# Wider idle matmuls, a split query load and one priority per step in a planned attention + MLP kernel

## The chip, the cores and the metric

One core of a Trainium2 chip. The metric is the device time of one execution in microseconds (us); every time below is of that kind or comes from one profiled execution. The engines are TensorE (PE, with PEld for its weight loads), VectorE (DVE), ScalarE (ACT), GpSimd (POOL) and SyncE (SP); they run side by side and wait for each other through semaphores. POOL issues the loads, SP the stores.

## The reference

```
batch, heads, seq, head_dim = 8, 8, 576, 64;  n_pack = 32
def sm_attn(qq, kk, vv):                     # softmax(qq kk^T / 8) vv
    ...
p_packed = sm_attn(p, k, v)                  # 32 packed rows per head
out = sm_attn(q, p_packed, p_packed)         # 576 rows per head
x = out.transpose(0, 2, 1, 3).reshape(8 * 576, 512)
r = maximum(x @ w_in, 0)                     # w_in 512 x 2048
result = (r * r) @ w_out                     # w_out 2048 x 512, float32
```

Inputs are float32; the kernel computes in bf16 with float32 sums.

## The kernel before

The kernel goes through the eight batches one after the other, with the eight heads of a batch in two halves of four ("qd" 0 and 1). A batch is a chain of steps, each with a short name, then the batch, then an index:

- `Lk`, `Lv`, `Lq`: loads of keys, values, queries, with a cast from float32 to bf16 on the way. `LWI.c.i` are the two halves of the four column chunks of w_in (order entries a0 to a3), `LWO.c` the eight chunks of two 128-row blocks of w_out (b0 to b7), `LP.2` the packed p of batches 2 to 7 (p2). Each is one `dma_start` on POOL.
- `Tk`, `Tq` (and `TR` for the rest of batch 0's queries): transposes on DVE (L458, L451, L455). `P`, `X`: p transposed and spread into block diagonals.
- `S1`: scores of p with the keys (PE, L467 to L482), then maximum (DVE, L490), exponential (ACT, L494), normalisation (DVE). `E`: transposes of it (PE, L507) and a copy. `PV`: times the values (PE, L521 and L541). `XT`: the packed rows copied out, turned and spread by small matmuls, and four small block copies into `pq_bd` (L373 on ACT or L375 on DVE).
- `S2` (for batch 0 `SA`, `SB`, `SC`; `ST`, `C` and `N` behind it): scores of q with the packed rows (PE, L629), transposes, maximum, subtraction, exponential, sum, product, transposes back.
- `M` (`MX`, `MY`, `MZ`): packed rows times w_in (PE, L596), so that the second attention's result need not be multiplied by w_in in full, and copies to SBUF.
- `F1` (batch 0: `FA` for its first 256 tokens, `F1` for the other 320): attention weights times `M` (PE, L782 and L795), relu (ACT mostly, L820 and L804), square (DVE mostly, L830).
- `F2.t.fb`: 128 tokens (tile t) times block fb of w_out (PE, L838, 512 columns, one matmul each), summed in one PSUM bank over fb 0 to 15; behind fb 15 a copy to `o_sb` and the stores. F2 blocks 2c and 2c+1 need load `LWO.c`. The last tile is done in three column parts (L855).

Nothing in this order is decided on the chip. While the program is built, the class `Plan` runs a list scheduler (`forward`, L68): streams of steps, a rough duration for each piece and engine, buffers and PSUM banks that must be free, and for every load a transfer time and a lag until it counts as landed (L894 to L904, L1117). Of the steps that can start, that with the lowest priority number goes first. The number is a step's base level plus an offset from the table `TABLE` (L248), looked up by the step's key (L205), which is the name up to the batch, so that all 16 matmuls of an F2 tile share one offset; a second table leans single pieces to or from ACT. Each engine then gets its instructions in the planned order and executes them strictly in that order.

Loads are issued in the order of `ORDER` (L1124), as far as the priorities leave it; at most eight are under way (the slot "dq", L874): the ninth is issued when the first has landed. Where the plan sees PE idle before the first F2, `fills` (L238) puts in matmuls on zeros into PSUM bank 7 (`keep_clock`, L357), 70 of them of 256 columns. The early lines of `ORDER`, up to `EARLY`, are streams of their own; the rest is one stream.

Of the kernel before, what the change touches and what calls it, by code (L numbers as in the profile page):

```python
# [53 lines left out]
class Plan:  # L54
# [147 lines left out]
    def aim(self):  # L202
        for steps in self.streams:
            for st in steps:
                st.prio = self.prio.get(st.key, self.level(st))  # L205
                st.late = st.prio - (50.0 if st.key[:2] == "F2" else 0.25)
                if st.key[0] == "L":
                    st.late = -200.0
                for stage in st.pieces:
                    for pc in stage:  # L210
                        pc.lean = self.lean.get(f"{st.key}/{pc.stage}", 0.0)
# [29 lines left out]
    def use(self, z):  # L241
        level = {st.key: self.level(st) for steps in self.streams for st in steps}
        self.prio = {k: level[k] + d for k, d in z.get("o", {}).items() if k in level}
        self.lean = z.get("l", {})
        self.wait, self.margin = z.get("w", 0.0), z.get("m", 0.0)


TABLE = {'o': {'P.0': 12.64, 'X.0': -182.5, 'P.2': 786.53, 'X.1': 824.47, 'La0': -989.93, 'La1': -654.2, 'La2':  # L248
# [54 lines left out]


def kernel_impl(tc, q, k, v, p, w_in, w_out, out):
# [922 lines left out]
```

## Time and profile before

| | |
|---|---|
| timed runs | 249.72 us median of 3 (249.71 to 249.84) |
| the profiled execution | 249.95 us, its span 248.2 us |
| granted TensorE clock, mean | 1.00 |
| PE busy | 234.0 us (94%), of which idle matmuls L359: 70 of 0.32 us |
| DVE, ACT, POOL busy | 193.1, 163.5, 43.0 us |
| chain that ended last, by engine | PE 71%, DMA 17%, DVE 4%, ACT 2% |
| F2, L838 | 509 records, 133.5 us |
| F1 of batches 1 to 7, L782 | 448 matmuls, 71.8 us; its relu on ACT 112 of 0.65 us, its square on DVE 112 of 0.46 us |
| load queue of POOL | 18.55 MB |

Busy times are unions: a matmul's record reaches beyond the start of the next one, so 0.379 us is the record of an F2 matmul and 0.213 us the distance to the next. A few per cent of the matmul records are missing, which shows as a gap of one matmul. The chain of waits is followed back from the last instruction, and a DMA piece in it lasts from issue to landing, with its time in the queue. The 40 slices of the page show where the load queue is full:

```profile
PE   7789799899999999999999999999999999999992
PEld 5465365356544654366544664466544654465452
DVE  7788989998799868996799669996799769756200
ACT  7457788969856597659756892567565793779110
POOL 8834544433343230000000000000000000000000
PEclk9999999999999999999999999999999999999999
DMA  6999999999999999702023111220032003310222
```

A digit is the busy share of 6.2 us in tenths. DMA is full for the first 16 slices, up to some 99 us; PE falls below 9 only in the first eight and the last.

### The profile page before, as it was taken

To read this page: it belongs to the slowest core of one execution; us is meant where nothing else is said; L and a number is where in the kernel's file an instruction comes from. 1 tells how busy PE (TensorE), PEld (TensorE's weight loads), DVE (VectorE), ACT (ScalarE), POOL (GpSimd) and SP (SyncE) were. 2 spreads that over 40 slices of the span, in tenths; PEclk is the share of its full clock that TensorE was granted. 3 is DMA by queue.
4 is the path that set the end of the run, shared out by engine and by line. 5 is a ranking of instruction groups with operands and counts; after the bars stand their busy time and mean duration, and the time that the engine had idled before them with its cause. 6 is when DMAs were issued, how large, how long until landed. Compare 5 with 4: busy or idle time off the path is not lost.

```text
span 248.2 us, 5863 instructions
## 1 busy us (share of the span) xinstructions
PE 234.0 (94%) x2315; PEld 129.9 (52%) x2350; DVE 193.1 (78%) x368; ACT 163.5 (66%) x284; POOL 43.0 (17%) x76
## 2 busy tenths in 40 slices
PE   7789799899999999999999999999999999999992
PEld 5465365356544654366544664466544654465452
DVE  7788989998799868996799669996799769756200
ACT  7457788969856597659756892567565793779110
POOL 8834544433343230000000000000000000000000
PEclk9999999999999999999999999999999999999999
DMA  6999999999999999702023111220032003310222
GB/s 106 202 191 207 202 203 203 203 228 241 223 220 224 237 217 207 189 21 66 0 66 80 29 42 43 57 64 13 3 87 66 21 0 85 86 44 0 68 72 75
DMA packets 26715, 28.50 MB, mean 115 GB/s; under 512 B 5440, under 2 KB 18112, under 8 KB 26688
## 3 DMA queue, kind: packets, MB, share of 16 engines
q0 software_dynamic: 18960, 18.55, 45.5%
q1 hardware_dynamic: 6960, 9.32, 13.6%
q8 instruction: 18, 0.29, 0.5%
q10 hardware_dynamic: 768, 0.26, 0.4%
q14 instruction: 9, 0.07, 0.1%
HBM read 37.22 MB, written 9.44 MB: 188 GB/s over the span
## 4 chain that ended last, share of the span: by engine, by line
PE 71%; DMA 17%; DVE 4%; issue 2%; POOL 2%; ACT 2%; SPq 0%; ACTq 0%; DVEq 0%; POOLq 0%
PE pb L838 41%; PE ps L782 21%; DMA w_in_b<-in_moe_w_in_dram 8%; DMA q_b<-in_q_dram 4%; DMA w_out_b<-in_moe_w_out_dram 4%; PE ps L596 2%; PE ps L482 1%; PE pb L507 1%; PE ps L629 1%; ACT r L820 1%; PE pb L521 1%; PE pb L629 1%; DMA out_dram<-o_sb 1%; DVE gT L830 1%; DVE n L753 1%
## 5 line engine op out<-in xcount | busy, mean ns | idle before, releaser
L838 PE MATMUL pb<-w_out_b,gT 128*128 128x512 bf16 x509 | 133.5, 379 | 3.1 <-issue 0.8
L838 PEld LDWEIGHTS <-gT 128*128 128x128 bf16 x560 | 51.9, 97 | 61.3 <-issue 6.5
L820 ACT ACTIVATE r<-ps 128x576 bf16<-128x576 f32 x112 | 71.9, 654 | 14.9 <-PE ps L782 10.3
L782 PE MATMUL ps<-a,M 128*128 128x288 bf16 x448 | 71.8, 286 | 0.4 <-ACT r L820 0.2
L830 DVE TENSOR_TENSOR gT<-r 128x576 bf16<-128x576 bf16 x112 | 50.8, 456 | 25.8 <-ACT r L820 24.7
L782 PEld LDWEIGHTS <-M 128*128 128x128 bf16 x448 | 43.1, 98 | 19.9 <-issue 1.4
L373 ACT COPY o_sb<-pb 128x512 f32<-128x512 f32 (+1 forms) x20 | 11.0, 555 | 24.0 <-PE pb L838 20.4
L373 ACT CAST M<-ps 128x1024 bf16<-128x1024 f32 (+1 forms) x20 | 19.2, 969 | 10.2 <-PE ps L596 10.1
L375 DVE COPY o_sb<-pb 128x512 f32<-128x512 f32 (+1 forms) x17 | 11.3, 662 | 10.8 <-PE pb L855 10.2
L494 ACT ACTIVATE e1x<-ps,n 128x576 bf16<-128x576 f32 x16 | 11.8, 739 | 10.5 <-DVE n L490 10.4
L741 ACT ACTIVATE e<-d 128x1152 bf16<-128x1152 f32 (+2 forms) x9 | 9.1, 1009 | 11.3 <-DVE d L736 11.3
L458 DVE STREAM_TRANSPOSE kT<-k_b 128x576 f32<-128x576 f32 x16 | 12.0, 775 | 2.3 <-DMA k_b<-in_k_dram 2.2
L428 POOL DMA_DIRECT2D v_b<-in_v_dram x16 | 11.2, 701 | 13.1 <-DMA k_b<-in_k_dram 5.7
L359 PE MATMUL pb<-zero 128*128 128x256 bf16 x70 | 11.7, 319 | 1.1 <-DVE zero L378 1.1
L490 DVE TENSOR_REDUCE n<-ps 128x1 f32<-128x576 f32 x16 | 11.5, 747 | 0.6 <-PE ps L482 0.5
L423 POOL DMA_DIRECT2D q_b<-in_q_dram x16 | 8.9, 562 | 17.1 <-DVE kT L458 5.2
L747 DVE TENSOR_REDUCE t<-e 128x36 f32<-128x1152 bf16 (+2 forms) x9 | 10.3, 1148 | 1.4 <-ACT e L741 1.4
L423 POOL DMA_DIRECT2D k_b<-in_k_dram x16 | 8.7, 543 | 13.5 <-DVE gT L830 3.3
L373 ACT CAST M<-pb 128x512 bf16<-128x512 f32 x18 | 9.9, 596 | 1.3 <-PE pb L596 1.3
L753 DVE TENSOR_TENSOR n<-e,r 128x1152 bf16<-128x1152 bf16 (+2 forms) x9 | 10.5, 1165 | 0.3
L451 DVE STREAM_TRANSPOSE qT<-q_b 128x576 f32<-128x576 f32 x14 | 10.7, 767 | 0.0
L645 DVE STREAM_TRANSPOSE a<-n 128x576 bf16<-128x576 bf16 (+1 forms) x14 | 10.1, 743 | 0.1
(103 smaller groups left out, 239.1 us busy)
## 6 DMA issues: line engine op xcount, KB each, us to landing
out_dram<-o_sb SPq DMA_DIRECT2D x141, 64.0 KB, 1.7
k_b<-in_k_dram POOLq DMA_DIRECT2D x16, 288.0 KB, 12.1
q_b<-in_q_dram POOLq DMA_DIRECT2D x16, 288.0 KB, 11.7
v_b<-in_v_dram POOLq DMA_DIRECT2D x8, 320.0 KB, 11.7
v_b<-in_v_dram POOLq DMA_DIRECT2D x8, 256.0 KB, 11.5
w_in_b<-in_moe_w_in_dram POOLq DMA_DIRECT2D x8, 256.0 KB, 10.8
w_out_b<-in_moe_w_out_dram POOLq DMA_DIRECT2D x8, 256.0 KB, 10.5
p_b<-in_p_dram POOLq DMA_DIRECT2D x1, 192.0 KB, 10.6
```

The costliest lines, as they stand in the source:

```text
L359: nc.tensor.matmul(half(7)[:, :2 * P], lhsT=zero[:, :P], rhs=zero, start=True, stop=True)
L373: nc.scalar.copy(dst, src)
L375: eng.tensor_copy(dst, src)
L423: nc.gpsimd.dma_start(t, src[self.b, qd * QH:(qd + 1) * QH].rearrange("h (a j) d -> (h a) (j d)", j=JT))
L458: nc.vector.transpose(kT[:, qd].rearrange("p s x -> p (s x)").bitcast(F32).rearrange("p (x a j2) -> p j2 x a", a=32, j2=2), self.t.k[qd][: ...
L490: nc.vector.tensor_reduce(self.n1[:, qd:qd + 1], self.ps1[qd], axis=AX.X, op=ALU.max, negate=True)
L494: nc.scalar.activation(e1x[:, qd], self.ps1[qd], ACT.Exp, bias=self.n1[:, qd:qd + 1], accum_out=self.d1[:, qd:qd + 1])
L753: eng.tensor_tensor(out=self.n2[:, g0:g1], in0=self.e2[:, g0:g1], in1=self.r2[:, g0:g1].unsqueeze(2).to_broadcast([P, g1 - g0, 32]), op=AL ...
L782: nc.tensor.matmul(ps[:, c], lhsT=a.M[:, qd, fb * FB:(fb + 1) * FB], rhs=a.a2[:, qd, c * HALF:(c + 1) * HALF], start=(qd == 0), stop=(qd = ...
L820: nc.scalar.activation(dst, src, ACT.Relu)
L830: eng.tensor_tensor(out=Att.cols(gT[:, fb, o:o + S]), in0=r, in1=r, op=ALU.mult)
L838: nc.tensor.matmul(po[t], lhsT=gT[:, fb, n0:n0 + P], rhs=w_out_b[:, fb, :], start=(fb == 0), stop=(fb == NFB - 1))
```

## The change

1. `keep_clock` pairs its idle matmuls: one of 512 columns for two of 256, the zeros read twice through a broadcast. The plan's count goes from 70 to 72 units of 256 columns, which makes 39 matmuls.
2. Batch 0's queries load in two token parts per half (`dma_qx`): tokens' first 8 of 18 groups (128 KB) in `Lq.0`, the other 10 (160 KB) in new steps `Lr.0`, behind the identity's set-up and ahead of w_in. `TR.0`, the transpose of the rest, waits for `Lr.0`.
3. The plan's lags until a load counts as landed become a table by kind of load (2.3 us to 3.3 us for most, 3.5 to 2.7 and 3.2 for w_in chunks 1 to 3), and the small copies of `XT` and the matmul of batch 0's `M` get longer planned durations.
4. Batch 0's attention steps may use PSUM bank 6 but no longer bank 7, into which the idle matmuls write.
5. Priorities are looked up by the step's full name first; the table has 960 offsets instead of 230.
6. The order that the plan makes of this differs on every engine. On POOL: w_in chunk 1 goes ahead of w_out chunks b0 and b2, p2 ahead of b3, and b5 ahead of b6. On PE, early: batch 0's second `PV` ahead of the first half's spread, and `S2.1.0` ahead of ten F2 matmuls. Pieces that change engine: the relus of F1.0.0, F1.0.3 and F1.0.4, the o_sb copy of F2 tile 2, the four block copies of XT.5, the M copy of MY.5 and two block copies of XT.7 go from DVE to ACT, one zeroing (I2.5) from ACT to DVE. PE's program has 62 rows fewer.

The diff, without the table's numbers:

```diff
-                st.prio = self.prio.get(st.key, self.level(st))
+                st.prio = self.prio.get(st.name, self.prio.get(st.key, self.level(st)))
...
-        level = {st.key: self.level(st) for steps in self.streams for st in steps}
+        level = {k: self.level(st) for steps in self.streams for st in steps for k in (st.name, st.key)}
...
         def keep_clock(n):
-            for _ in range(n):
-                nc.tensor.matmul(half(7)[:, :2 * P], lhsT=zero[:, :P], rhs=zero, start=True, stop=True)
+            for i in range(0, n, 2):
+                w = min(2, n - i)
+                nc.tensor.matmul(half(7)[:, :w * 2 * P], lhsT=zero[:, :P], rhs=zero[:, None, :].to_broadcast([P, w, 2 * P]), start=True, stop=True)
...
+            def dma_qx(self, qd, j0, j1):
+                if qd not in self.q:
+                    self.q[qd] = qkv.tile([P, JT * D], BF16, name="q_b", tag="kqb")
+                nc.gpsimd.dma_start(self.q[qd][:, j0 * D:j1 * D],
+                                    q[self.b, qd * QH:(qd + 1) * QH].rearrange("h (a j) d -> (h a) (j d)", j=JT)[:, j0 * D:j1 * D])
...
-            lag=lag or (LAG0 if name[1:4] in ("k.0", "v.0", "q.0") else LAG))
+            lag=lag or LAGS.get(name[1:4], LAG))
...
-            return [load_step(f"LWI.{fq}.{cp}", 1.3, ..., 0.71, LAG + (1.2 if fq else 0.0)) for cp in range(2)]
+            return [load_step(f"LWI.{fq}.{cp}", 1.3, ..., 0.71, 3.2 if fq > 1 else None) for cp in range(2)]
...
-                        Step(f"TR.0.{qd}", ..., [f"Tq.0.{qd}"], (), [("kqb", 0, f"Lq.0.{qd}")]) for qd in QDS]
+                        Step(f"TR.0.{qd}", ..., [f"Tq.0.{qd}", f"Lr.0.{qd}"], (), [("kqb", 0, f"Lq.0.{qd}")]) for qd in QDS]
...
-                                                     [[("DVE", 0.15, ... block_solo ...), ("ACT", 0.15, ...)] for h in range(QH)]],
+                                                     [[("DVE", 0.22, ... block_solo ...), ("ACT", 0.21, ...)] for h in range(QH)]],
...
-                                     [[("DVE", 0.22, ... pq_block ...), ("ACT", 0.21, ...)] for h in range(QH)]],
+                                     [[("DVE", 0.3, ... pq_block ...), ("ACT", 0.265, ...)] for h in range(QH)]],
...
-                        res.append(Step(nm, [[[("PE", 0.19, ... m ...)]],
+                        res.append(Step(nm, [[[("PE", 0.235, ... m ...)]],
...
-                           [f"XT.{b}.{x}", f"Tq.{b}.{x}"], banks=AB + OB, free=[(2, None)]) for x in range(2)]
+                           [f"XT.{b}.{x}", f"Tq.{b}.{x}"], banks=AB + OB[:1], free=[(2, None)]) for x in range(2)]
...
-        LAG0, LAG = 1.75, 2.3
+        LAG = 3.3
+        LAGS = {"k.0": 1.92, "v.0": 2.5, "q.0": 2.5, "r.0": 2.6, "WI.": 2.7, "k.1": 2.7, "WO.": 2.8}
...
-        EARLY = 21
-        ORDER = ("k0 v0 q0 i0 a0 a1 a2 a3 b0 b1 k1 b2 b3 v1 b4 b5 q1 b6 b7 p2 "
+        EARLY = 22
+        ORDER = ("k0 v0 q0 i0 r0 a0 a1 a2 a3 b0 b1 k1 b2 b3 v1 b4 b5 q1 b6 b7 p2 "
...
-            if x[0] in "kq":
+            if x == "q0":
+                g = [load_step(f"Lq.0.{qd}", 0.63, lambda qd=qd: L[0].dma_qx(qd, 0, 8), [("kqb", 1)]) for qd in QDS]
+            elif x == "r0":
+                g = [load_step(f"Lr.0.{qd}", 0.79, lambda qd=qd: L[0].dma_qx(qd, 8, JT)) for qd in QDS]
+            elif x[0] in "kq":
```

More of the change, by code (lines that the diff above doesn't have):

```diff
@@ L245, in use @@
         self.wait, self.margin = z.get("w", 0.0), z.get("m", 0.0)
-TABLE = {'o': {'P.0': 12.64, 'X.0': -182.5, 'P.2': 786.53, 'X.1': 824.47, 'La0': -989.93, 'La1': -654.2, 'La2':
[54 rows of a table removed]
+TABLE = {'o': {'P.0': 457.35, 'X.0': 851.54, 'P.2': -259.11, 'X.1': -213.12, 'Lr0': -1432.02, 'La0': -1345.04,
[202 rows of a table added]
 def kernel_impl(tc, q, k, v, p, w_in, w_out, out):
@@ L890, in load_step @@
         def load_step(name, us, fn, slot=[], issue=0.56, lag=None):
-            return Step(name, [[[("POOL", issue, fn)]], [[("DMA", us, lambda: None)]]], (), slot + [("dq", 1)], [("dq", 1, None)], lag=lag or (LAG0 if name[1:4] in ("k.0", "v.0", "q.0") else LAG))
+            return Step(name, [[[("POOL", issue, fn)]], [[("DMA", us, lambda: None)]]], (), slot + [("dq", 1)], [("dq", 1, None)], lag=lag or LAGS.get(name[1:4], LAG))
         def load_kq(b, nm):
@@ L900, in load_wi @@
         def load_wi(fq):
-            return [load_step(f"LWI.{fq}.{cp}", 1.3, lambda cp=cp: dma_w_in(fq, cp), [], 0.71, LAG + (1.2 if fq else 0.0)) for cp in range(2)]
+            return [load_step(f"LWI.{fq}.{cp}", 1.3, lambda cp=cp: dma_w_in(fq, cp), [], 0.71, 3.2 if fq > 1 else None) for cp in range(2)]
         def load_wo(cs):
@@ L914, in tr_steps @@
                 return [Step(f"Tq.0.{qd}", [[[("DVE", 0.36, lambda qd=qd: T[0].tr_qx(qd, 0, 2 * P))]]], [f"Lq.0.{qd}"]) for qd in QDS] + [
-                        Step(f"TR.0.{qd}", [[[("DVE", 0.43, lambda qd=qd: T[0].tr_qx(qd, 2 * P, S))]]], [f"Tq.0.{qd}"], (), [("kqb", 0, f"Lq.0.{qd}")]) for qd in QDS]
+                        Step(f"TR.0.{qd}", [[[("DVE", 0.43, lambda qd=qd: T[0].tr_qx(qd, 2 * P, S))]]], [f"Tq.0.{qd}", f"Lr.0.{qd}"], (), [("kqb", 0, f"Lq.0.{qd}")]) for qd in QDS]
             return [Step(f"T{nm}.{b}.{qd}", [[[("DVE", 0.7, lambda qd=qd: (T[b].tr_k if nm == "k" else T[b].tr_q)(qd))]]],
@@ L948, in pv_steps @@
                     res.append(Step(n1, [[[("PE", 0.33, lambda qd=qd, n1=n1: T[b].pv_solo(qd, U[n1]))]]],
-                                    [f"E.{b}.{qd}", f"Lv.{b}.0", f"Lv.{b}.1", "I"], (), [("vb", 0, f"Lv.{b}.0")] if qd else [], banks=AB + OB, mode=1))
+                                    [f"E.{b}.{qd}", f"Lv.{b}.0", f"Lv.{b}.1", "I"], (), [("vb", 0, f"Lv.{b}.0")] if qd else [], banks=AB + OB[:1], mode=1))
                     res.append(Step(f"XT.{b}.{qd}", [NO, [[("DVE", 0.15, lambda qd=qd: T[b].extract_solo(qd, V)),
@@ L952, in pv_steps @@
                                                      [[("PE", 0.085, lambda qd=qd: T[b].spread_solo(qd))]],
-                                                     [[("DVE", 0.15, lambda h=h, qd=qd: T[b].block_solo(qd, h, V)),
-                                                       ("ACT", 0.15, lambda h=h, qd=qd: T[b].block_solo(qd, h, A))] for h in range(QH)]],
+                                                     [[("DVE", 0.22, lambda h=h, qd=qd: T[b].block_solo(qd, h, V)),
+                                                       ("ACT", 0.21, lambda h=h, qd=qd: T[b].block_solo(qd, h, A))] for h in range(QH)]],
                                     [n1], free=[(3, n1)]))
@@ L962, in pv_steps @@
                                      [[("PE", 0.115, lambda: T[b].spread())]],
-                                     [[("DVE", 0.22, lambda h=h: T[b].pq_block(h, V)),
-                                       ("ACT", 0.21, lambda h=h: T[b].pq_block(h, A))] for h in range(QH)]],
+                                     [[("DVE", 0.3, lambda h=h: T[b].pq_block(h, V)),
+                                       ("ACT", 0.265, lambda h=h: T[b].pq_block(h, A))] for h in range(QH)]],
                          [nm], free=[(5, nm)])]
@@ L972, in m_steps @@
                         nm = f"M.{b}.{c}.{x}"
-                        res.append(Step(nm, [[[("PE", 0.19, lambda c=c, x=x, nm=nm: T[b].m(c, U[nm], 0, [x]))]],
+                        res.append(Step(nm, [[[("PE", 0.235, lambda c=c, x=x, nm=nm: T[b].m(c, U[nm], 0, [x]))]],
                                              [[("ACT", 0.49, lambda c=c, x=x: T[b].m_half(c, x, A)),
@@ L1032, in s2_steps @@
                                    [[("DVE", 0.55, lambda x=x: T[b].one_sum(x))]], [[("DVE", 0.34, lambda x=x: T[b].one_mul(x))]]],
-                           [f"XT.{b}.{x}", f"Tq.{b}.{x}"], banks=AB + OB, free=[(2, None)]) for x in range(2)]
+                           [f"XT.{b}.{x}", f"Tq.{b}.{x}"], banks=AB + OB[:1], free=[(2, None)]) for x in range(2)]
                 hs.append(Step(hn[2], [[[("PE", 0.45, lambda: T[b].s2_half(1, U[hn[2]]))]]] + front(1, 512) + chain(1, 512),
-                               pre, banks=AB + OB, free=[(2, None)]))
+                               pre, banks=AB + OB[:1], free=[(2, None)]))
                 nr = f"SC.{b}.2"
-                return [hs[0], hs[1], hs[2], nstep(0, hn[:2], AB + OB), Step(nr, [[[("PE", 0.12, lambda: T[b].s2_rest(U[nr]))]]] + front(2, 128) + chain(2, 128),
-                                                     pre, banks=AB + OB, free=[(2, None)], mode=1), nstep(1, [hn[2], nr], AB + OB)]
+                return [hs[0], hs[1], hs[2], nstep(0, hn[:2], AB + OB[:1]), Step(nr, [[[("PE", 0.12, lambda: T[b].s2_rest(U[nr]))]]] + front(2, 128) + chain(2, 128),
+                                                     pre, banks=AB + OB[:1], free=[(2, None)], mode=1), nstep(1, [hn[2], nr], AB + OB[:1])]
             if b in TURNED:
```

256 rows, old and new, of the table TABLE are left out of this document.

## The prediction

> **What bounds the kernel now.** I read the table of stages first, cut where the waits of TensorE change.
>
> ```profile
> core 0: us, PE busy (x) PEld busy (x) DVE busy (x) ACT busy (x) POOL busy (x), PEclk, DMA share, GB/s
> 0.00:25.00 25.00, 20.25 (x198) 13.45 (x200) 19.11 (x51) 15.25 (x34) 15.53 (x32) 1.00 1.08 177
> 25.00:48.67 23.67, 21.29 (x229) 11.02 (x232) 21.29 (x40) 19.98 (x34) 11.43 (x18) 1.00 1.31 202
> 48.67:240.17 191.50, 189.00 (x1843) 102.26 (x1874) 152.25 (x278) 127.15 (x216) 16.03 (x27) 1.00 0.47 98
> ```
>
> From 48.67 us to the last matmul's end, TensorE (PE) is busy 189.00 of 191.50 us at a granted clock of 1.00. All that any reordering can win back there is 2.50 us, and missing matmul records make up part of that. So the end is fixed by when PE enters this stretch and by how much work is then left. Next, the chain that ended last:
>
> ```profile
> 27.42 10.62 DMA q_b<-in_q_dram
> 38.03 0.28 issue
> 38.32 10.31 DMA w_out_b<-in_moe_w_out_dram
> 48.62 0.04 issue
> 48.67 0.59 PE pb L838 x2
> ```
>
> Columns: start, duration, what. Before 48.67 us the chain is loads: each waits some 10 us in the queue behind those ahead of it. The last weight chunk (w_out rows of fb 14 and 15, "b7") lands at 48.62 us. PE's timeline shows that it came too late:
>
> ```profile
> 39.31 0.59 PE L838 MATMUL pb<-w_out_b,gT 128*128 128x512 bf16 x2
> ...
> 47.66 0.38 PE L838 MATMUL pb<-w_out_b,gT 128*128 128x512 bf16 x1 [0.16 <-issue]
> 48.67 0.59 PE L838 MATMUL pb<-w_out_b,gT 128*128 128x512 bf16 x2 [0.63 <-DMA w_out_b<-in_moe_w_out_dram]
> ```
>
> Last, POOL's timeline. A load is issued when the load eight places ahead has landed, so each row dates a landing: start minus 0.29 us, since the landings at 38.03 and 48.62 us free the issues at 38.32 and 48.91.
>
> ```profile
> 17.07 0.71 POOL L431 DMA_DIRECT2D w_in_b<-in_moe_w_in_dram  x1 [0.62 <-DMA w_in_b<-in_moe_w_in_dram]
> 19.61 0.70 POOL L431 DMA_DIRECT2D w_in_b<-in_moe_w_in_dram  x1 [1.83 <-DMA w_out_b<-in_moe_w_out_dram]
> ...
> 32.59 0.70 POOL L435 DMA_DIRECT2D w_out_b<-in_moe_w_out_dram  x1 [0.53 <-DMA v_b<-in_v_dram]
> 34.21 0.70 POOL L435 DMA_DIRECT2D w_out_b<-in_moe_w_out_dram  x1 [0.92 <-DMA v_b<-in_v_dram]
> ...
> 39.55 0.72 POOL L428 DMA_DIRECT2D v_b<-in_v_dram  x1 [0.53 <-DMA w_out_b<-in_moe_w_out_dram]
> 40.84 0.68 POOL L428 DMA_DIRECT2D v_b<-in_v_dram  x1 [0.57 <-DMA p_b<-in_p_dram]
> ...
> 48.91 0.69 POOL L428 DMA_DIRECT2D v_b<-in_v_dram  x1 [0.73 <-DMA w_out_b<-in_moe_w_out_dram]
> ```
>
> Chunk b3 lands at 39.26 us, and PE first uses it at 39.31. The load of p for batches 2 to 7 (p2) lands at 40.55, b7 at 48.62.
>
> **The change part by part.** *Idle matmuls.* The first 22 of 256 columns take 4.82 us (0.219 each); 11 of 512 columns are the same columns. All stand before S1.1.0, which waits for batch 1's keys anyway (the row at 24.67 us dates that landing to 24.38, the transpose takes 0.78). A wider one can delay a useful matmul by another 0.11 us (half of 0.219). Cost: 0, under that cover.
>
> *Split q load.* Batch 0's queries become four loads of 128 and 160 KB for two of 288. Bytes are equal; the question is a fixed part per load. From landings: v loads of 256 and 320 KB land 1.23 and 1.62 us after the one before (rows 31.37, 32.59, 34.21), at least in proportion, so a fixed part of 0. Against that, 288 KB take 1.41 (12.21 to 13.62) and 256 KB 1.33 (20.71 to 22.04): 0.08 us for 32 KB, and a fixed part of 1.33 - 8 x 0.08 = 0.69 us. Bounds for two added loads: 0 and 1.38 us on every later landing. I take 0.10, near the v rows, which are like with like. The two more issues on POOL (0.56 us each, in front of the w_in loads) cost nothing: the first w_in load, issued at 6.84, waits until 15.46 us to land.
>
> The Trainium skill ("DMA: Bandwidth & Descriptors", section "Anatomy of one DMA — SWDGE (gpsimd) path") gives each such load about 2.0 us of fixed time, mostly the wait for the write's receipt. Landings 1.23 us apart disagree that it is paid in line; if it were, two loads would cost 4.0 us, and the sum would be 254.1 us.
>
> *Order at the start.* PE now runs PV.0.1 ahead of XT.0.0's matmul, and ACT copies two of half 0's four blocks, all of half 1's, then half 0's last two: eight of 0.21 us instead of four ahead of the first scores. They can begin after about 13.4 us, so SA.0.0 moves from 13.91 to about 15.2 us, N.0.0 from 18.91 to some 20.4, and four FA steps of about 0.5 end near 23. S1.1.0 cannot start before 24.38 + 0.78 + 0.1 = 25.25 us in either kernel: some 2 us of cover. By S1.1.1 the sets of steps done are the same again. From there to PV.1.0 (34.06 us; its v half lands at 33.92 in both orders) nothing is won. Cost 0; without the cover, what exceeds 2 us.
>
> *p2 ahead of b3; S2.1.0 earlier.* This is the term that decides. b3 now lands where p2 did: 40.55 + 0.10 + 0.05 for PE to react, 40.70 us. PE would be there at about 39.9: before needs 5.25 us from PV.1.0 (34.06) to b3's first use (39.31), and after has FA.0.6 (four matmuls of 256 columns, 0.43) and S2.1.0 (0.76) more in between and three F2 matmuls (0.64) fewer, 5.80 us. So it waits. Before needs from 39.31 to 47.66 + 0.21 = 47.87 us, 8.56 us, to reach b7's first use. After has S2.1.0 out of this stretch (41.14 to 41.90 in PE's timeline, -0.76) and 29 instead of 27 F2 matmuls (+2 x 0.213): 8.23 us. 40.70 + 8.23 = 48.93. b7, behind the same bytes, lands at 48.72 + 0.05: no longer the last to come. PE enters the full stretch at 48.93 instead of 48.67: +0.26.
>
> *Work left there.* At b7's first use 41 F2 matmuls are done instead of 42, all else equal: +0.21.
>
> *From there on.* The priority table only permutes work on a full PE. DVE hands ACT three relus (about 0.7), four and two block copies (0.255 each in ACT's rows), one M copy (0.97) and one o_sb copy (0.58); ACT is busy 127 of 191 us and DVE 152. I take 0; bounds -2.50 (the idle time) and +1.5 (below).
>
> Sum: +0.26 + 0.21 = +0.47 on the profiled execution's 249.95 us (span 248.2 and 1.75 around it), so 250.42. The three timed runs have a median of 249.72, 0.23 below it: **250.2 us**. By the terms' own bounds 249.8 to 250.8.
>
> **Rivals.**
> *A, faster: the late step in the queue is not repeated.* Landings follow each other by 1.1 to 1.6 us, but the one of 19.32 comes 2.54 after that of 16.78 (rows 17.07, 19.61), about 1.2 late, and nothing later makes it up. In the window 16.5 to 19.5 us the DMA view has one packet of 16 KB of the instruction queue, which the page lists with 18 packets in all. With PE's program 62 rows shorter, that packet comes elsewhere; if not on the engine that lands last, every later landing is 1.2 us earlier. It decides only if PE also gets to b3 earlier than 39.9 us, which it can if S1.1.1 is spared the 0.59 us that it waits at 28.16 for a PSUM bank: b3 used from 39.5, + 8.23 = 47.73, 0.94 earlier than 48.67, and +0.21 of work left: -0.7, 249.0 us. Against: the packet comes all the same.
> The skill ("Runtime: NRT & Kernel Launch", section "Instruction fetch mechanics") calls crossing a 16 KiB block mostly hidden. PE has no wait there; the landing behind it is the late one, and that the packet causes it is not shown.
>
> *B, slower: ACT becomes the bound in batches 4 to 6.* XT.5's four block copies, on DVE before, go to ACT between relus of F1.4 that PE needs for its two PSUM pairs. S2.5.0 follows eight F2 matmuls (1.71 us) after the last F1.4, and ACT then still has a relu and two copies, 0.65 + 2 x 0.255 = 1.16: a cover of 0.5. If ACT is later than that, each of the six copies moved (XT.5, XT.7) can stop PE for its 0.255: +1.5 and the +0.47: 251.7 - 0.23 = 251.5, less if part is covered. For it: ACT at 9.1 of 10 us in 220:230. Against: ACT at 5.1 in 150:160.
>
> *C, no change:* p2 does not decide, since b3's first use comes later than I read; PE waits for b7 as before, +0.10 + 0.21: 250.0.
>
> *D, slower: the fixed part is real.* 0.69 us on each added load: b3 at 41.98, PE at 50.21, +1.54 + 0.21: 251.5. Against: the v rows.
>
> **How the numbers follow.** The forecast gets 0.40, A 0.22, B 0.17, C 0.13, D 0.08. A measurement tells about 0.2% (0.5 us) from no change, so 249.2 and 250.2 are the edges. The forecast lies on the upper one: 0.21 slower, 0.19 same. A: 0.20 faster, 0.02 same. C: same. B and D: slower. Faster 0.20, same 0.34, slower 0.46. The range 248.9 to 251.4 holds the forecast, C and about half of each of the others; the forecast's own is 249.8 to 250.6.
>
> **What would show it.** Right: the first F2 matmul on b3's rows waits for DMA w_out_b near 40.7 us; b7's first use comes without a long wait near 48.9; the stretch behind it is 191.7 us long. Wrong in the load term: landings behind the split q load over 0.3 us later (D), or 1 us earlier (A). Wrong in the last part: ACT r or ACT pq_bd named in front of PE's L782 or L629 with sums over 0.5 us after 140 us (B), or a last stretch shorter than 191.3 us. The forecast is wrong altogether if PE enters the full stretch more than 0.8 us from 48.9.

## The result and the profile after

| | before | after |
|---|---|---|
| timed runs, median | 249.78 us (249.13 to 249.94) | 248.33 us (247.78 to 248.55) |
| ratio | | 0.9944, 95% interval 0.9929 to 0.9958 |
| the profiled execution | 249.95 us, span 248.2 us | 248.32 us, span 246.5 us |
| PE, DVE, ACT busy | 234.0, 193.1, 163.5 us | 237.2, 188.6, 166.7 us |

The change makes the kernel 0.56% faster; a time 0.2% longer was forecast. PE's busy time can't be compared: before's trace has 2315 of 2350 matmul records, after's has all 2319. In after's code, lines behind the table stand 155 later (L838 is now L993, L782 L937, L629 L784, L830 L985, L375 L524, L373 L522).

The table of stages of after, cut where PE enters the full stretch; columns as in the prediction:

```profile
0.00:25.00 25.00, 21.47 (x164) 10.07 (x165) 18.96 (x51) 14.54 (x33) 17.16 (x34) 0.93 1.09 177
25.00:48.44 23.44, 21.52 (x237) 11.18 (x235) 20.29 (x39) 22.09 (x37) 11.03 (x17) 1.00 1.31 202
48.44:239.14 190.70, 190.70 (x1875) 102.69 (x1875) 148.95 (x269) 128.93 (x224) 16.09 (x27) 1.00 0.47 98
```

The cut at 239.14 us (ACT's copy of the last full tile) answers to before's 240.17. That was not the last matmul's end, as the prediction has it: the last tile's column parts run on behind it. PE enters it 0.23 us earlier and it is 0.80 us shorter, with no idle time left in the records. The granted clock of 0.93 in the first 25 us is not the change's: after_again, the same kernel, has 1.00 there, and order_late and lanes_before, with the early program of before, have 0.93. The chain of waits of after, as far as the entry:

```profile
26.31 10.62 DMA q_b<-in_q_dram
36.92 0.28 issue
37.21 11.19 DMA w_out_b<-in_moe_w_out_dram
48.44 0.38 PE ps L993
```

It is the chain of before: b7 lands last, at 48.39 us, although the loads ahead of it landed earlier than before, most by about a microsecond, the one just ahead by 0.56. POOL's timeline dates that (start minus 0.29 us):

```profile
17.78 0.70 POOL L586 DMA_DIRECT2D w_in_b<-in_moe_w_in_dram  x1 [0.57 <-DMA w_in_b<-in_moe_w_in_dram]
19.66 0.71 POOL L586 DMA_DIRECT2D w_in_b<-in_moe_w_in_dram  x1 [1.18 <-DMA w_in_b<-in_moe_w_in_dram]
...
46.91 0.70 POOL L583 DMA_DIRECT2D v_b<-in_v_dram  x1 [1.34 <-DMA k_b<-in_k_dram]
48.68 0.69 POOL L583 DMA_DIRECT2D v_b<-in_v_dram  x1 [1.06 <-DMA w_out_b<-in_moe_w_out_dram]
```

Where before has a step of 2.54 us (17.07 to 19.61), after has one of 1.88; another, of 1.77 us, stands just ahead of b7 (46.91 to 48.68).

Three rows of the timeline split both spans: S2.3.0's first matmul, where both kernels have done the same PE steps; DVE's copy of the last tile's first column part; the end.

| | before | after | difference |
|---|---|---|---|
| to S2.3.0 | 95.89 us | 95.83 us | -0.06 |
| S2.3.0 to DVE's last copy (the stretch) | 146.09 | 145.11 | -0.98 |
| from there to the end of the span (the end) | 6.20 | 5.60 | -0.60 |

So in this pair the early part, on which the forecast rests, did nothing, and the gain stands where the forecast had a zero and no term at all.

### The profile page after: what moved, and what is told of

It is laid out like the page before. It is cut to its first block, busy times and chain, and to the rows that moved or that the text cites. A ratio compares the mean times of both kernels' runs of the same rounds, so it can differ in the third digit from the quotient of the medians.

```text
span 246.5 us, 5839 instructions
## 1 busy us (share of the span) xinstructions
PE 237.2 (96%) x2319; PEld 127.1 (52%) x2319; DVE 188.6 (77%) x358; ACT 166.7 (68%) x294; POOL 44.3 (18%) x78
## 4 chain that ended last, share of the span: by engine, by line
PE 77%; DMA 17%; POOL 3%; issue 1%; ACT 0%; SPq 0%; ACTq 0%; POOLq 0%
PE pb L993 46%; PE ps L937 23%; DMA w_in_b<-in_moe_w_in_dram 7%; DMA w_out_b<-in_moe_w_out_dram 5%; DMA q_b<-in_q_dram 4%; PE ps L751 2%; PE ps L637 2%; PE ps L784 1%; PE pb L662 1%; PE pb L676 1%; POOL q_b L577 1%; DMA out_dram<-o_sb 1%; PE pb L751 1%; POOL k_b L572 0%; ACT o_sb L522 0%
## 5 line engine op out<-in xcount | busy, mean ns | idle before, releaser
L993 PE MATMUL pb<-w_out_b,gT 128*128 128x512 bf16 x544 | 137.4, 380 | 0.4 <-ACT gT L966 0.4
L993 PEld LDWEIGHTS <-gT 128*128 128x128 bf16 x560 | 52.0, 98 | 60.4 <-issue 6.3
L975 ACT ACTIVATE r<-ps 128x576 bf16<-128x576 f32 x112 | 70.6, 652 | 14.1 <-PE ps L937 10.7
L985 DVE TENSOR_TENSOR gT<-r 128x576 bf16<-128x576 bf16 x112 | 51.1, 457 | 28.4 <-ACT r L975 26.3
L937 PE MATMUL ps<-a,M 128*128 128x288 bf16 x448 | 70.2, 286 | 0.0
L937 PEld LDWEIGHTS <-M 128*128 128x128 bf16 x448 | 42.9, 98 | 19.6 <-issue 0.9
L522 ACT CAST M<-ps 128x1024 bf16<-128x1024 f32 (+1 forms) x20 | 19.5, 992 | 12.7 <-PE ps L751 12.6
L522 ACT COPY o_sb<-pb 128x512 f32<-128x512 f32 (+1 forms) x21 | 11.6, 558 | 23.9 <-PE pb L993 20.5
L524 DVE COPY o_sb<-pb 128x512 f32<-128x512 f32 (+1 forms) x16 | 10.5, 664 | 10.3 <-PE pb L1010 8.0
L508 PE MATMUL pb<-zero 128*128 128x512 bf16 (+1 forms) x39 | 13.1, 470 | 1.1 <-DVE zero L527 1.1
L572 POOL DMA_DIRECT2D q_b<-in_q_dram x14 | 7.8, 557 | 17.0 <-DVE kT L613 5.8
L522 ACT CAST M<-pb 128x512 bf16<-128x512 f32 x19 | 10.7, 591 | 0.2 <-PE pb L751 0.2
```

The lines of the kernel that those rows point to most:

```text
L508: nc.tensor.matmul(half(7)[:, :w * 2 * P], lhsT=zero[:, :P], rhs=zero[:, None, :].to_broadcast([P, w, 2 * P]), start=True, stop=True)
L522: nc.scalar.copy(dst, src)
L572: nc.gpsimd.dma_start(t, src[self.b, qd * QH:(qd + 1) * QH].rearrange("h (a j) d -> (h a) (j d)", j=JT))
L937: nc.tensor.matmul(ps[:, c], lhsT=a.M[:, qd, fb * FB:(fb + 1) * FB], rhs=a.a2[:, qd, c * HALF:(c + 1) * HALF], start=(qd == 0), stop=(qd = ...
L975: nc.scalar.activation(dst, src, ACT.Relu)
L985: eng.tensor_tensor(out=Att.cols(gT[:, fb, o:o + S]), in0=r, in1=r, op=ALU.mult)
```

## The experiments

All times in us; "before" ran beside each on the same chip and gave 249.41 to 249.53.

| kernel | median | ratio to before (95%) | to S2.3.0 | stretch | end |
|---|---|---|---|---|---|
| order_late | 248.16 | 0.9938 to 0.9967 | 95.46 | 145.30 | 5.60 |
| order_early | 249.51 | 0.9994 to 1.0026 | 95.93 | 145.82 | 5.98 |
| after_again | 248.26 | 0.9928 to 0.9967 | 95.65 | 145.09 | 5.61 |
| idle_256 | 248.18 | 0.9935 to 0.9967 | 95.82 | 145.11 | 5.61 |
| q_whole | 248.17 | 0.9940 to 0.9964 | 95.62 | 145.10 | 5.60 |
| b3_ahead | 248.37 | 0.9937 to 0.9969 | 95.42 | 145.11 | 5.61 |
| xt_dve | 248.77 | 0.9955 to 0.9985 | 95.91 | 145.65 | 5.62 |
| xt_act | 248.87 | 0.9950 to 0.9985 | 94.93 | 145.57 | 5.89 |
| xt5_act | 248.69 | 0.9951 to 0.9983 | 95.52 | 145.54 | 5.91 |
| lanes_before | 248.66 | 0.9962 to 0.9988 | 94.82 | 145.81 | 5.64 |
| lanes_after | 248.81 | 0.9952 to 0.9984 | 95.95 | 145.12 | 5.97 |
| s27_one | 249.48 | 0.9989 to 1.0020 | 96.29 | 146.06 | 6.18 |
| xt_act_lanes | 248.65 | 0.9950 to 0.9983 | 95.64 | 145.60 | 5.62 |
| three_parts | 248.48 | 0.9933 to 0.9969 | 95.51 | 145.50 | 5.63 |
| b7_ahead | 248.87 | 0.9963 to 0.9993 | 97.19 | 145.09 | 5.60 |
| b7_tk | 248.34 | 0.9930 to 0.9969 | 96.27 | 145.09 | 5.60 |

The stretch, end and start are from one trace of each kernel. In after and the seven kernels that share its order from S2.3.0 to DVE's last copy, on the same engines, the stretch repeats to 0.03 us (145.09 to 145.12). It is not always the code's alone: order_late has the same late order and 145.30, and the order of before shows two values, 145.8 and 146.1 (both are placed at the end of "S2.7" below). The start varies by more than a microsecond.

**Which half holds the gain.** The plan's order was written out as a list, with engines and PSUM banks, and two lists were joined at S2.3.0:

```diff
     def run(self):
-        out, T = self.forward()
-        for p in sorted(out, key=lambda p: p.start):
+        for x in SEQ.split():    # one list up to S2.3.0, then what is left of the other
...
```

order_late:

> Order of before on every engine up to S2.3.0 (95.9 us), the order and the engine choices of after behind it; loads and idle matmuls as before. Theory S (the gain comes from the order behind 96 us: 0.99 us less idle time on PE there, and 0.63 us less from the last tile's first matmul to the end): 248.2 to 248.8 us. Theory L (the gain comes from the early part, whose loads land 1.1 us earlier): no gain, 249.6 to 250.0 us.

order_early:

> The mirror image: loads, idle matmuls and order of after up to S2.3.0, the order of before behind it. Theory S: within 0.2 us of before, 249.6 to 250.0 us, with PE's waits for gT in batch 5 (0.23 and 0.16 us) and for ACT's r (0.16 us) back. Theory L: 248.2 to 248.5 us, like after.

after_again:

> The changed kernel once more, unchanged. 248.3 us. If the 0.63 us at the end belong to the order, the time from the last tile's first matmul to the end of the span is 7.6 us again (8.2 us before); if they are chance, it lies elsewhere between 7.5 and 8.3 us. If the stretch's smaller idle time belongs to the order, PE again has no wait over 0.1 us behind 51 us.

All three came out as theory S has it, order_early and order_late with medians 0.1 and 0.04 us below the ranges given. Behind before's early part with its loads, after's late order gives the whole gain within the intervals; behind after's early part, before's late order gives none. Order_early's interval, -0.15 to +0.65 us, leaves no room for an early gain that matters, but some for a small early loss. Both halves of the gain go with the late order, the end too, though its code is the same in both kernels.

**The parts of the forecast, undone one by one in after.**

```diff
 idle_256
-            for i in range(0, n, 2):
-                w = min(2, n - i)
+            for w in [1] * n:
 q_whole
-  dma_qx(qd, 0, 8) in Lq.0; dma_qx(qd, 8, JT) in Lr.0
+  dma_qx(qd, 0, JT) in Lq.0; nothing in Lr.0
 b3_ahead (in run)
+        seq.insert(at("LP.2"), seq.pop(at("LWO.3")))
```

idle_256:

> After, with its 72 idle units as single matmuls of 256 columns again; nothing else. PE's program gets 66 rows longer. If the 16 KB packet of the instruction queue causes the late landing of the second w_in load, that landing comes 2.5 us behind the one before it again, b3 lands near 40.6 us, PE waits for b3 about 1.2 us, and the time is 248.5 to 249.2 us. If the packet is not the cause, landings are those of after within 0.2 us and the time is 248.3 us.

q_whole:

> After, with batch 0's queries in one load per half again, at the places of the first parts. By the prediction's own term (0.10 us for two loads) and by rival D (0.69 us each) every later landing comes 0.1 or 1.4 us earlier than in after; b7 lands at 48.3 or 47.0 instead of 48.2 to 48.4, PE enters the full stretch as much earlier. By the new reading (a late step of some 1 us comes in every run at another place and b7 lands at 48.2 to 48.6 us all the same): within 0.2 us of after, 248.1 to 248.4 us.

b3_ahead:

> After, with the load of b3 issued ahead of that of p2 again, as before the change. If b3's landing decides when PE enters the full stretch (the deciding term of the prediction), b3 lands 1.2 us earlier and the time is 0.2 to 0.4 us less than after's 248.2: 247.8 to 248.0 us. If b7 decides, whatever comes ahead of it: 248.1 to 248.4 us, with PE's wait at b7 near 48.4 us and none at b3.

None of the three moves the time. In idle_256 PE's program has 66 rows more, yet the step of 2.5 us between two landings does not come back at its place (1.88 us there, 1.12 behind it); one of 2.2 us comes at 44 us. In order_late, with before's early program word for word, the step comes one load later (17.79 to 20.11) and the next landing follows after 1.00 us. After and after_again, one and the same program, have their longest steps at 19.37 us (1.88) and 37.78 us (2.62). So the late step is not tied to the program: it comes somewhere in each execution. The Trainium skill ("Runtime: NRT & Kernel Launch", section "Instruction fetch mechanics") calls a block's crossing mostly hidden; these runs agree, in that 66 rows more leave the time at 248.18 us, against after_again's 248.26. q_whole has two loads fewer and b7 lands at 48.09, against 48.39 in after and 48.20 in after_again: no fixed part of 0.69 us each. The 2.0 us that the Trainium skill's "DMA: Bandwidth & Descriptors" (section "Anatomy of one DMA — SWDGE (gpsimd) path") gives one load are not paid one behind the other here either. In b3_ahead b7 landed early, at 47.6, PE has no wait for it, and the median is still after's; the 0.2 to 0.4 us that the deciding term would win did not come.

**The stretch: the engine of the block copies.**

```diff
             e, us, fn = p.alts[p.alt]
+            if p.stage == 5 and (p.step.name == "XT.5" or p.step.name == "XT.7" and p.k < 2):
+                e, us, fn = p.alts[0]      # xt_dve, on after: DVE
+            if p.stage == 5 and p.step.name in ("XT.5", "XT.7"):
+                e, us, fn = p.alts[1]      # xt_act, on before: ACT; xt5_act: XT.5 alone
```

xt_dve:

> After, with the four block copies of XT.5 and two of XT.7 on DVE again, where they were before; the order is unchanged. Rival B of the prediction (these copies on ACT stop PE) makes this kernel the same or faster than after: 248.2 us or less. The new reading (with the copies on DVE the scores S2.5 and S2.7 come late: S2.7's first matmul to the first F2 behind it takes 1.25 us in the order of before and 0.95 in that of after) makes it slower than after by 0.3 to 0.5 us: 248.5 to 248.8 us, with the wait back in front of S2.7.

xt_act:

> Before, with the block copies of XT.5 (four) and XT.7 (the two that DVE had) on ACT and nothing else. Rival B of the prediction: ACT stops PE, 0 to 1.5 us slower, 249.4 to 250.9 us. The new reading: the scores S2.5 and S2.7 no longer wait for copies queued on DVE, S2.7's stage takes 0.95 us instead of 1.25, and the time is 0.4 to 0.6 us less than before's 249.4: 248.8 to 249.0 us.

xt5_act:

> Before, with the four block copies of XT.5 on ACT and nothing else (XT.7 stays as it was). From S2.3.0's first matmul to DVE's copy of the last tile's first column part, looks at the order of before gave 145.8 us, at that of after 145.1, at xt_act 145.6. If XT.5 does the good of xt_act and XT.7 none: 145.5 us, F2.22's wait for gT near 164 us gone, S2.7's stage still 1.25 us. If XT.7 was needed: 145.7 us or more.

Taking the copies back to DVE costs after 0.54 us of stretch (145.65). Giving them to ACT wins the order of before 0.25, measured from its 145.82, all of it XT.5's (145.54). xt_dve's median is as far from after's as expected, though the two intervals overlap. The reason is in the table of stages, cut from XT.5 to the first F2 matmul of tile 22. Before:

```profile
147.60:165.00 17.40, 17.07 (x174) 8.24 (x176) 17.07 (x29) 8.46 (x15) 0.00 (x0) 1.00 0.18 47
```

The same stage in xt5_act, where XT.5's copies are the one edit, and the same 17.40 us of after, whose order of work differs:

```profile
147.20:164.60 17.40, 17.13 (x176) 8.35 (x178) 16.55 (x26) 9.47 (x19) 0.00 (x0) 1.00 0.18 47
147.60:165.00 17.40, 17.40 (x177) 8.34 (x175) 16.08 (x27) 10.67 (x20) 0.00 (x0) 1.00 0.15 39
```

In this stage DVE is busy 17.07 of 17.40 us before and ACT 8.46: the shares of the whole stretch (152 and 127 of 191 us) do not show it. What leaves DVE here lets what is behind it start earlier. Before, at the stage's end:

```profile
164.19 0.65 PE L782 MATMUL ps<-a,M 128*128 128x288 bf16 x4
164.43 0.42 DVE L830 TENSOR_TENSOR gT<-r 128x576 bf16<-128x576 bf16 x1
164.90 0.39 PE L838 MATMUL pb<-w_out_b,gT 128*128 128x512 bf16 x1
```

The same place in xt5_act (two lines later in its code):

```profile
163.54 0.46 DVE L832 TENSOR_TENSOR gT<-r 128x576 bf16<-128x576 bf16 x1
163.73 0.65 PE L784 MATMUL ps<-a,M 128*128 128x288 bf16 x4
164.22 0.38 PE L840 MATMUL pb<-w_out_b,gT 128*128 128x512 bf16 x1
```

F2.22 needs the square of F1.5.0, which DVE ends at 164.85 before: PE, 0.71 us behind the first matmul of F1.5.1, stood 0.22 us. In xt5_act the square is done at 164.00, and F2 follows 0.49 us behind that first matmul, without a wait. S2.5 gains too: from its first matmul to the first F2 behind it takes 0.11 us less.

**S2.7.** The scores need all four copies of XT.7. The timeline of before:

```profile
204.64 0.58 DVE L375 CAST pq_bd<-pb 32x128 bf16<-32x128 f32 x2
205.31 0.53 ACT L373 CAST pq_bd<-pb 32x128 bf16<-32x128 f32 x2 [0.38 <-DVE pq_bd L375]
205.59 0.30 PE L629 MATMUL ps<-qT,pq_bd 64*32 64x288 bf16 x1
205.89 0.28 PE L629 MATMUL pb<-qT,pq_bd 64*32 64x288 bf16 x1
```

and of after:

```profile
203.11 0.65 ACT L975 ACTIVATE r<-ps 128x576 bf16<-128x576 f32 x1
203.66 1.06 ACT L522 CAST pq_bd<-pb 32x128 bf16<-32x128 f32 x4
205.07 0.30 PE L784 MATMUL ps<-qT,pq_bd 64*32 64x288 bf16 x1
```

Before, one matmul starts at 205.59 and the rest wait until 205.89 for copies that end at 205.84. After, the copies end at 204.72, 0.35 us ahead of S2.7. (S2.7's stage of 1.25 and 0.95 us, in the expectations and below, counts from 0.22 us behind the start of the F2 matmul ahead of it; from S2.7's own first matmul it is 0.10 less.) Two single edits failed to give that. xt_act left S2.7's stage at 1.30 us, where 0.95 was expected: its four copies (1.06 us) follow F1.6's last relu, which starts 1.30 us ahead of S2.7, in after 1.96. So one F2 matmul was moved ahead of S2.7:

```diff
+        seq.insert(at("S2.7.0"), seq.pop(at("F2.28.15")))
```

s27_one:

> Before, with one F2 matmul (F2.28.15, 0.213 us) moved on PE from behind S2.7.0 to ahead of it. If S2.7 is late because PE comes to it before the block copies of XT.7 are done, and not because of the engine that does them: S2.7's stage takes 0.2 us less (1.04 instead of 1.25) and the stretch 145.6 instead of 145.8 us. If PE's place is not the point: 145.8 us.

No gain: F2.28.15 needs the last square of F1.6. In three_parts, which has the same edit, S2.7's wait is gone (0.96 us instead of 1.25), but the moved matmul starts 0.26 us late, 0.06 behind that square's end. The wait changed its place. What does it in after is left to PE's new order around F1.6 as a whole; no smaller edit was found.

Order_early's trace has every matmul record, so its 0.71 us over after (145.82 to 145.11) can be placed: PE stands 0.22 us at F2.22 and 0.30 at S2.7, and the stages of S2.5 and S2.6 are 0.12 and 0.08 longer. The 0.27 that before and s27_one have on top of it stand at one place: F1 matmuls at 172.91 us in before follow a relu that ACT begins at 172.21, 0.29 us behind its copy, where order_early, with the same order, has it at 171.97; so the wait for ACT's r that was expected back in order_early did not come. Order_late's 0.2 over after stand at F1 matmuls at 168.9 us, likewise behind a relu that ACT begins 0.23 us later than in after_again. The profiles do not show what ACT waits for in these places.

**The end.** Before, from the timeline:

```profile
241.98 0.42 DVE L375 COPY o_sb<-pb 128x256 f32<-128x256 f32 x1 [10.18 <-PE pb L855]
...
244.77 0.56 ACTq L861 DMA_DIRECT2D out_dram<-o_sb  x1
```

After:

```profile
240.94 0.42 DVE L524 COPY o_sb<-pb 128x256 f32<-128x256 f32 x1 [8.02 <-PE pb L1010]
...
243.49 0.57 ACTq L1016 DMA_DIRECT2D out_dram<-o_sb  x1
```

From the last store's issue to the end (248.18 and 246.54) before takes 3.41 us, after 3.05. The trace's semaphore rows of SP say why: the stores signal eight semaphores in turn, and SP's last act is to wait for them one after the other in a fixed order (semaphore, time passed):

```
before: last ACT store signals 109   109 246.85  112 246.91  113 246.98 ... 117 247.22  118 247.28
after:  last ACT store signals 117   109 244.16  112 244.45  113 245.33 ... 117 245.60  118 245.66
```

Before, the store that lands last signals the first of the eight, and seven more steps of 0.06 us come after it. After, most steps are done while that store is under way. (The other 0.24 us lie ahead of the store, 2.79 us behind DVE's copy before and 2.55 after; only before and s27_one have them.) To shift the turn, a few stores were split:

```diff
-                eng.dma_start(dst, ob[t][32 * i:32 * i + 32, o])
+                for c in (slice(0, 256), slice(256, NE)) if 40 <= 4 * t + i < 46 else (o,):
+                    eng.dma_start(dst[:, c], ob[t][32 * i:32 * i + 32, c])
```

(46 in before; 42 in after.)

lanes_before:

> Before, with six of the 32-row stores of tiles 10 and 11 done in two column halves, so that six more stores shift the eight store semaphores, and the very last ACT store signals semaphore 117 (as in after) instead of 109. If the end of the program is shorter because SP's closing row of semaphore checks no longer stands at its second check until that store has landed: from the last tile's first matmul to the end 7.6 us instead of 8.0 to 8.2, and 0.35 to 0.6 us less in all, 248.9 to 249.2 us against 249.4 to 249.7. If the end is a matter of chance or of PE's order: 8.0 to 8.2 us again, and no gain.

lanes_after:

> The mirror image of lanes_before: after, with two of the 32-row stores done in two column halves, so that the last ACT store signals semaphore 109 as in before. If SP's closing checks cost the time: the end from DVE's last copy 5.9 to 6.2 us instead of 5.6, and 248.5 to 248.8 us in all. If not: 5.6 us and 248.2 us.

Both ends moved as expected, 5.64 with semaphore 117 in before's program (5.98 with 109 in order_early), 5.97 with 109 in after's. (In lanes_before SP's own last store signals 109, and the end is 0.04 above after's.) The medians moved too, by more than the 0.35 us of the end: lanes_before's 248.66 lies below the 248.9 to 249.2 expected, lanes_after's 248.81 at the upper edge. How much more is within their scatter.

**Together, on before, without the rest of the change:**

xt_act_lanes:

> Before, with xt_act's edit and the six split stores of lanes_before; neither the idle matmuls, nor the split query load, nor any priority of the change. If the copies' engine and the last store's semaphore are the two main causes of the gain: 248.2 to 248.6 us, that is 0.8 to 1.2 us less than before. If the order of PE, of the loads or of the start is needed for it: 249.0 us or more.

three_parts:

> Before, with three edits alone: XT.5's copies on ACT, F2.28.15 ahead of S2.7.0, and the six split stores. If these are the causes: the stretch 145.3 us (after 145.1, before 145.8 to 146.1), the end from DVE's last copy 5.6 us (before 6.0 to 6.2), and 248.4 to 248.7 us in all, at least two thirds of the gain. If the gain needs the rest of the new order: 249.0 us or more.

Both medians are 0.9 us below before's, and three_parts' ratio is within the interval of after. But the medians do not add up: xt_act alone has nearly the interval of xt_act_lanes, and xt5_act and lanes_before each take some 0.7 us off alone. The traces do: stretch and end of three_parts together are 0.67 us shorter than order_early's, of 1.09 that after has. XT.5's engine (0.28) and the last store's semaphore (0.35) are thus more than half of the gain, and a stretch of 145.3 was missed (145.50). The 0.39 us of stretch that three_parts lacks against after stand mostly at F2.28.15 (0.26) and in S2.6's stage (0.09); moving F2.28.15 adds nothing.

**A faster one?** b7 is last to come, so it was issued ahead of batch 2's keys:

```diff
+        seq.insert(at("Lk.2.0"), seq.pop(at("LWO.7")))
+        seq.insert(at("Tk.2.1") - 1, seq.pop(at("Tk.2.0")))    # b7_tk only
```

b7_ahead:

> After, with the last chunk of w_out (b7) issued ahead of the two loads of batch 2's keys. If b7's landing at 48.4 us is what PE's 0.38 us of idle time at 48.44 waits for: b7 lands near 45.5 us, PE has no wait there, and the time is 247.8 to 248.0 us. If the keys, 1.4 us later each, become the next wait (the transposes of 0.7 us and S1.2 behind them at 50.9 us), the gain is given back there: 248.2 us or more.

b7_tk:

> After, with b7 ahead of batch 2's keys as in b7_ahead, and the transpose Tk.2.0 moved on DVE behind batch 1's sum and product (C.1), next to Tk.2.1. In b7_ahead DVE stood 2.0 us at Tk.2.0 with C.1 queued behind it. If that was all: PE has no wait at b7, S1.2 starts near 50.6 instead of 50.9 us, and the time is 247.8 to 248.0 us. If S1.2 or F1.1 still waits for DVE: 248.2 us or more.

b7_ahead loses what it should have won. DVE's timeline:

```profile
47.67 0.78 DVE L616 STREAM_TRANSPOSE kT<-k_b 128x576 f32<-128x576 f32 x1 [2.01 <-DMA k_b<-in_k_dram]
48.37 1.31 DVE L905 TENSOR_REDUCE t<-e 128x36 f32<-128x1152 bf16 x1
```

DVE stood at the keys' transpose with batch 1's sum behind it, 2.36 us later than in after (46.01); S1.2 follows at 51.80 instead of 50.90. That VectorE's queue is strictly first in, first out is stated by the Trainium skill ("PSUM — Partial Sum Buffer", section "Engine vs sequencer instructions"), and these rows agree: the sum starts 0.70 us behind the transpose that stood. b7_tk removes that wait and PE has none left from 38 to 53 us, yet S1.2 starts at 51.05 and the time is after's. None of the kernels is shown to beat after.

## Why the prediction was wrong

- **Idle matmuls 0, start order 0 under 2 us of cover:** right. S1.1.0 starts at 25.20 us (25.25 before), S1.1.1 at 28.09 (28.16); SA.0.0 at 15.57 and N.0.0 at 20.71, foreseen 15.2 and 20.4.
- **Split q load +0.10:** right in size, and without effect. From the landing of batch 0's last values to that of its last queries, nine traces with two loads have 2.76 us in the mean (2.61 to 2.80), nine with four have 2.88 (2.75 to 2.96): +0.12. At the first w_in load nothing of it is left (4.28 and 4.20 us), and the time of q_whole is after's.
- **p2 ahead of b3, the deciding term, +0.26:** did not happen. b3 landed at 39.51, not 40.65; PE waits for no w_out chunk ahead of b7 and enters at 48.44, not 48.93. The step behind it took one execution's landings as the queue's: their steps of 1.1 to 1.6 us hold, but the late one wanders. b7 lands between 47.4 and 48.6 us in all kernels that leave its place, with either order of the loads.
- **One F2 more left, +0.21:** right as a count; with the entry's -0.23 it comes to nothing. (From one F2 matmul to the next takes 0.216 us in both traces, not 0.213.)
- **"From there on ... I take 0":** the step that failed. Measured: -0.98 us in the pair, -0.7 against order_early. The prediction's own sign of it came: its last stretch is 190.70 us long, below 191.3. The term's bounds (-2.50 to +1.5) held it, but the ranges given for the time leave out most of them. The value was chosen from shares of busy time over 191 us, and rival B priced the moves by ACT's queue alone. In the 17 us behind XT.5, DVE was 98% busy and ACT 49%; in the 150:160 us for which B quotes ACT's 5.1, DVE was busy 9.80. The same pieces on the same timeline, read by stage, had the sign. B's own place (S2.5, XT.7) was right, its sign wrong; its time is also 0.2 us too low, since 251.7 already has the 0.23 taken off.
- **No term for the end:** "its span and what lies around it" was carried over, and the end of the span had a different length, -0.60 us in the pair and about -0.35 by the semaphore alone.
- **Rival A** saw the landings come a microsecond earlier, but not from the program's length, and b7 gave it back; that its 249.0 lies nearest to the result is luck. **C** had the entry right: p2 did not decide, and PE waited for b7 as before (0.48 us). Its +0.3 is not shown, and order_early cannot exclude it. **D** fell with the landings: 0.12 us for two loads, not 1.38.

The sum of the measured terms, -0.06 - 0.98 - 0.60, is the -1.64 us between the spans.

Open: what ACT waited for in the late relu of before and s27_one, and why just these two also have an end of 6.2 us; whether the early part costs a few tenths; and which of PE's moves around F1.6 frees S2.7.

## What to carry to other kernels

When pieces move between engines, read each engine's busy share in the stage where they move, not over the whole run: here the engine that was full there decided the sign. A landing time from one profile is one draw; a forecast that hangs on one load being 0.3 us earlier than another needs more than one trace. And the end of a program is a stage too: look at what the last store's completion still has to pass.

## What the runs showed of the hardware

- The closing waits of SP cost 0.06 us a step in a fixed order, and which semaphore the last store signals decided 0.34 us of the end in the program of before (5.98 to 5.64) and 0.37 in that of after (5.60 to 5.97).
- Two loads more for the same bytes delayed the landing of the last of them by 0.12 us in the mean of nine traces each.
- With eight loads under way, landings mostly follow each other by 1.1 to 1.6 us, but each of the 18 traces has a step of 1.86 to 2.85 us between 16 and 52 us, at one load or another. The next landing makes up 0.8 us of it in after_again and 0.2 in before. The longest step ends at 19.3 us in before (2.54 us), at 19.8 in order_late (2.32), at 37.8 in after_again (2.62), at 44.1 in idle_256 (2.18).
